# A gated recurrence with a highway layer on one Trainium2 core: the leftover tokens on 96 partitions, another order of the loads inside a tile, and a new instruction list

## The chip, the cores and the metric

The kernel runs on one core of a Trainium2 chip. The metric is device time in microseconds (us) of one execution; lower is better. Inputs and output are in HBM, in float32.

The engines are named as the profile names them. PE is the matrix engine, and PEld its weight loads. DVE, ACT and POOL are the three elementwise engines. SP computes nothing and only issues transfers. Transfers (DMA) are carried out by 16 DMA engines; the profile calls the share of their time that is busy the DMA share, with 1 for all 16.

## What is computed

```
sig = 1 / (1 + exp(-f_logit))                # f_logit, x: (4, 6336, 256)
f = lower_bound + (1 - lower_bound) * sig    # lower_bound: (256)
h = 0
for t in range(6336):                        # per batch and channel
    h = f[:, t] * h + (1 - f[:, t]) * x[:, t];  y[:, t] = h
y = y.reshape(25344, 256)
H = max(y @ w_h, 0);  T = 1 / (1 + exp(-(y @ w_t + b_t)))
out = T * H + (1 - T) * y                    # (25344, 256)
```

The recurrence runs along the tokens of a batch; the four batches are independent. The two inputs and the output have 25.95 MB each.

## The kernel before, in words

**Units.** The tokens are cut into 29 units (UNITS). Each row names k, the runs of tokens (batch, first token, number), the split of the product e between two engines, and how the steps are grouped. Most units are one run of 1024 tokens with k = 8; the first five and the last two are shorter (256 or 512 tokens). Since 6336 is not a multiple of 1024, one unit differs from the rest: unit 15 takes 192 tokens of each of the four batches, 768 tokens, with k = 6.

**Token layout.** A unit is loaded with k neighbouring tokens on each of the 128 partitions: token p*k + j lies on partition p, place j. A full unit is a load of 1 MB for f_logit (tile l) and one of 1 MB for x (tile x), in which each partition receives 8 KB that are contiguous in HBM. Unit 15 has 32 partitions for each batch and 6 KB on each partition. Its HBM side is a pattern with the four batches outermost (`in_dram`, line 219).

**Steps of a unit n**, each named by a letter in the list OPS:

- l, x: the two loads, and o: the stores (two of 512 KB for a full unit). All are issued by SP (lines 223 and 381).
- U (ACT, line 259): u = sigmoid(-l). B (POOL, line 281; DVE in the first two units, line 279): bv = u*x.
- T (PE, line 287): u is transposed, so that channels lie on partitions and tokens along a row; k transposes of 128 columns for each of the two halves h of the channels. F (ACT, line 297): f is made out of the transposed u; its read pattern (`token_order`, line 225) puts the tokens into their natural order. V (PE, line 305): the same transpose for bv, written in the natural order directly, two tokens at a time.
- S (DVE, line 313): the recurrence along the tokens. It needs the last column of the unit before in the same batch.
- Z and G (PE, line 324): the two products with the weights. A (ACT, line 335): the gate t. D (DVE, line 339): d = max(...) - y. E (DVE, line 345) and P (POOL, line 352): e = d*t, in two parts.
- O (PE, lines 363 and 364): y and e are transposed back and added, in PSUM (the accumulator memory that PE writes). C (ACT, line 376): the result is copied to the tile o, which the store sends out.

**Order.** OPS is one long written list. Each engine works through its own items in exactly that order, and SP issues loads and stores in that order too, each after the waits that its buffers need. The part behind the @ names the buffer: there are four l and four x buffers, three u and three bv, five y, eight o, four PSUM banks s and two double banks pp. X items are matmuls on zeros that only keep PE busy early on.

Of the kernel before, what the change touches and what calls it, by code (L numbers as in the profile page):

```python
# [36 lines left out]
    (6, ((0, 3072, 192), (1, 3072, 192), (2, 3072, 192), (3, 3072, 192)), 384, (4, 2), (2, 2, 2), (4, 2), ()),  # L37
# [23 lines left out]
X4@s0 Tb@s0 cst l0@l0 x0@x0 W1 W0 U0.0@u0 B0.0@bv0 X1@s1 T0.0@s1 T0.1@s2 F0.1@f0 F0.0@f1 w1 l1@l1 U1.0@u1  # L61
V0.0@s3 V0.1@s0 dia v1 S0.0@y0 X7@s2 T1.0@s2 S0.1 w0 v0 l2@l2 x1@x1 F1.0@f2 U2.0@u2 T1.1@s1 X3@pp0 Z0.0@pp0
X1@s3 T2.0@s3 F1.1@f3 A0.0@t0 B1.0@bv1 V1.1@s2 S1.1@y1 T2.1@s0 G0.0@pp1 Z0.1@pp0 V1.0@s1 D0.0@d0 X1@pp1
G0.1@pp1 S1.0 F2.0@f1 F2.1@f0 A0.1 x2@x2 B2.0@bv2 l3@l3 l4@l0 U3.0@u0 x3@x3 l5@l1 B3.0@bv0 X1@pp0 Z1.1@pp0
D0.1 A1.1@t1 U4.0@u1 G1.1@pp1 D1.1@d1 V2.0@s3 T3.1@s2 T3.0@s0 Z1.0@pp0 G1.0@pp1 S2.0@y2 F3.1@f3 F3.0@f2
V2.1@s1 S2.1 X1@s3 T4.1@s3 T4.0@s2 F4.1@f1 A1.0 F4.0@f0 D1.0 E1@e0 E0@e1 X4@pp1 G2.0@pp1 D2.0@d1 x4@x0 x5@x1
l6@l2 U5.0@u2 V3.0@s0 Z2.1@pp0 V3.1@s1 O0.0@s3 Z2.0@pp1 S3.0@y3 S3.1 A2.1@t1 A2.0 T5.1@s2 T5.0@s0 G2.1@pp0
C0.0@o0 F5.1@f2 D2.1 B4.0@bv1 B5.1@bv2 B5.0 Z3.0@pp1 V4.0@s1 O1.0@s3 Z3.1@pp0 V4.1@s2 A3.0@t0 F5.0@f3 A3.1
U6.0@u0 G3.1@pp1 G3.0@pp0 C1.0@o1 S4.0@y4 S4.1 D3.1@d0 D3.0 E2@e1 E3@e0 x6@x2 l8@l3 l7@l0 x7@x3 x8@x0 o0.0
o1.0 l9@l1 x9@x1 Z4.0@pp1 V5.0@s1 T6.0@s0 S5.0@y0 A4.0@t1 F6.0@f0 B6.0@bv0 B6.1 Z4.1@pp0 A4.1 O2.0@s2 O3.1@s3  # L70
C3.1@o2 U8.0@u1 C2.0@o3 V5.1@s0 G4.1@pp1 T6.1@s3 G4.0@pp0 S5.1 D4.0@d1 D4.1 V6.0@s1 U7.0@u2 F6.1@f1 Z5.0@pp0
T8.1@s0 V6.1@s2 Z5.1@pp1 S6.0@y1 B7.1@bv1 B7.0 A5.0@t0 F8.1@f3 A5.1 O3.0@s3 G5.1@pp0 T7.1@s1 S6.1 D5.1@d0
T7.0@s0 G5.0@pp1 E4@e0 D5.0 F7.1@f2 C3.0 F7.0@f0 Z6.1@pp0 V7.0@s2 A6.1@t1 U9.0@u0 O2.1@s1 O4.1@s3 V7.1@s0
Z6.0@pp1 B8.0@bv2 B8.1 S7.0@y3 S7.1 E5@e1 A6.0 T8.0@s2 G6.1@pp0 G6.0@pp1 T9.0@s0 C2.1 C4.1@o4 F8.0@f1 F9.0@f0
O4.0@s1 V8.1@s3 O5.2@s2 C4.0 C5.2@o5 l13@l2 l10@l3 U10.0@u2 x10@x2 l11@l0 D6.0@d1 D6.1 B9.1@bv0 B9.0 S8.1@y2
E6@e0 G7.1@pp1 T9.1@s0 O5.1@s1 Z7.0@pp0 D7.1@d0 T10.1@s2 V8.0@s3 C5.1@o6 F9.1@f2 A7.0@t0 F10.1@f3 O5.0@s1 C5.0
U11.0@u1 V9.0@s0 G7.0@pp0 Z7.1@pp1 O6.1@s2 C6.1@o7 x11@x3 o3.0 l12@l1 l17@l3 x12@x0 x13@x1 o2.0 S8.0 B10.0@bv1
B10.1 B11.1@bv2 O5.3@s1 D7.0 T11.0@s3 V9.1@s2 A7.1 P7.0@e1 B11.0 Z8.1@pp0 F11.0@f1 C5.3 A8.1@t1 S9.0@y4 S9.1
Z8.0@pp1 O6.3@s3 O6.2@s1 A8.0 T10.0@s0 G8.1@pp0 G8.0@pp1 O6.0@s2 C6.3@o0 U13.0@u0 C6.2 C6.0 F10.0@f0 D8.1@d1
D8.0 E7 E8@e0 V10.1@s3 Z9.0@pp0 S10.1@y0 O7.3@s1 A9.0@t0 C7.3@o1 T11.1@s2 F11.1@f2 V10.0@s0 G9.1@pp1 O7.0@s1  # L80
C7.0@o2 D9.1@d0 U12.0@u2 Z9.1@pp0 O7.2@s3 C7.2 S10.0 V11.0@s2 G9.0@pp1 V11.1@s1 O7.1@s3 T13.0@s0 A9.1 C7.1
F13.0@f3 Z10.1@pp0 D9.0 P8.0 B13.0@bv0 B13.1 B12.1@bv1 P9.0@e1 B12.0 T12.0@s3 G10.0@pp1 O8.2@s0 A10.1@t1
Z10.0@pp0 F12.0@f0 C8.2@o3 A10.0 l14@l0 o6.0 x17@x2 o7.0 o5.0 x14@x3 l15@l2 O8.3@s3 C8.3 x15@x1 o8.1 o4.0
S11.0@y1 D10.0@d1 S11.1 O8.1@s2 O8.0@s0 C8.1@o7 C8.0 U14.0@u1 G10.1@pp1 T13.1@s3 G11.1@pp0 T12.1@s2 D10.1 E9
E10@e0 D11.1@d0 V12.0@s1 Z11.0@pp1 O9.3@s0 S12.0@y3 F12.1@f1 F13.1@f2 A11.0@t0 C9.3@o2 Z11.1@pp0 O9.0@s2
V12.1@s3 S12.1 C9.0@o6 A11.1 B14.1@bv2 P10.0 B14.0 U15.0@u0 V13.0@s0 O9.2@s1 C9.2 O9.1@s2 G11.0@pp1 C9.1
U17.0@u2 G12.0@pp0 T14.1@s3 V13.1@s1 o8.0 l16@l1 o5.1 x16@x0 o9.0 x18@x3 l19@l0 D11.0 D12.0@d1 B15.0@bv1
P11.0@e1 S13.1@y2 S13.0 E11 Z12.1@pp1 G12.1@pp0 F14.1@f0 T15.1@s2 T14.0@s3 O10.3@s1 A12.1@t1 Z12.0@pp1
F14.0@f1 C10.3@o3 V14.0@s3 O10.1@s1 O10.2@s0 A12.0 Z13.1@pp1 C10.1@o4 F15.1@f2 A13.1@t0 C10.2 O11.2@s1
O10.0@s2 D12.1 S14.0@y4 B17.1@bv0 B15.1 P12.0@e0 G13.1@pp0 D13.1@d0 C11.2@o7 C10.0 U16.0@u1 O11.3@s0 T15.0@s1  # L90
V14.1@s3 C11.3 O11.0@s2 F15.0@f3 C11.0@o5 Z13.0@pp1 G13.0@pp0 O11.1@s0 A13.0 B16.1@bv2 S14.1 D13.0 E12 E13@e1
P13.0 B16.0 B17.0 T16.0@s1 T17.1@s3 V15.0@s2 C11.1 F16.0@f1 F17.1@f0 o9.1 l18@l2 o7.1 o6.1 l24@l3 o11.1 l20@l1
x19@x1 o10.1 S15.0@y0 Z14.1@pp0 Z14.0@pp1 O12.3@s0 V15.1@s1 O12.0@s3 T17.0@s2 A14.1@t1 C12.3@o6 A14.0 S15.1
G14.1@pp0 O12.1@s0 G14.0@pp1 D14.1@d1 D14.0 O12.2@s1 C12.0@o2 U18.0@u0 C12.2 C12.1 F17.0@f3 G15.1@pp0 V16.0@s3
P14.0@e0 D15.1@d0 S16.0@y1 E14 Z15.1@pp1 O13.2@s1 C13.2@o1 T16.1@s0 F16.1@f2 O13.0@s2 Z15.0@pp0 V16.1@s1
C13.0@o0 A15.1@t0 A15.0 V17.0@s0 O14.0@s3 C14.0@o7 S16.1 G15.0@pp1 O13.3@s2 O14.2@s3 O13.1@s1 D15.0 U19.0@u2
C13.3 B18.0@bv1 B18.1 P15.0@e1 B19.1@bv2 S17.0@y3 C13.1 C14.2@o3 Z16.0@pp0 G16.0@pp1 A16.0@t1 T18.0@s2
V17.1@s1 T18.1@s3 O14.1@s0 D16.0@d1 S17.1 F18.0@f1 G16.1@pp0 Z16.1@pp1 F18.1@f2 C14.1 A16.1 V18.0@s2 T19.1@s3
T19.0@s0 O14.3@s1 F19.1@f3 C14.3 F19.0@f0 D16.1 E15 E16@e0 S18.0@y2 P16.0 B19.0 Z17.0@pp1 V18.1@s3 O15.1@s1
G17.1@pp0 O15.0@s0 o12.1 l22@l2 o13.0 o11.0 x20@x0 l21@l0 o12.0 o14.1 x23@x2 x22@x3 x21@x1 o10.0 D17.1@d0  # L100
S18.1 A17.0@t0 C15.1@o6 U20.0@u1 C15.0 G17.0@pp1 O16.0@s2 C16.0@o0 Z17.1@pp0 A17.1 D17.0 T20.1@s1 O16.2@s0
O15.2@s2 V19.0@s3 B20.0@bv0 B20.1 P17.0@e1 Z18.0@pp0 C16.2@o5 C15.2@o2 F20.1@f1 A18.0@t1 G18.0@pp1 O16.3@s0
C16.3 O16.1@s2 V19.1@s1 S19.0@y4 D18.0@d1 S19.1 E17 U21.0@u0 Z18.1@pp0 V20.1@s3 T20.0@s0 G18.1@pp1 A18.1 C16.1
F20.0@f2 Z19.0@pp0 D18.1 S20.1@y0 B21.1@bv1 B21.0 P18.0@e0 A19.0@t0 O17.0@s1 T21.1@s2 F21.1@f0 U22.0@u2
V20.0@s0 G19.0@pp1 D19.0@d0 S20.0 G19.1@pp0 C17.0@o3 T21.0@s2 O17.3@s3 C17.3@o4 Z19.1@pp1 F21.0@f3 T22.1@s1
O17.1@s3 O17.2@s2 V21.1@s0 A19.1 D19.1 E18 E19@e1 o15.1 o15.0 x24@x0 l23@l1 l26@l0 C17.2 o17.1 o16.1 o16.0
S21.1@y1 Z20.1@pp1 C17.1 F22.1@f1 V21.0@s2 O18.1@s3 Z20.0@pp0 A20.1@t1 C18.1@o2 A20.0 S21.0 U23.0@u1 B22.0@bv2
P19.0 G20.0@pp1 O18.0@s1 O18.2@s3 G20.1@pp0 T22.0@s0 O18.3@s2 C18.0 C18.2@o6 C18.3 B22.1 D20.0@d1 D20.1
O19.2@s1 G21.1@pp1 U24.0@u0 F22.0@f2 C19.2@o4 D21.1@d0 B23.1@bv0 P20.0@e0 B23.0 x25@x1 l25@l2 o14.0 x26@x3
l28@l1 o17.0 o18.1 o13.1 o18.0 l27@l3 T23.0@s3 V22.1@s2 Z21.0@pp0 G21.0@pp1 V22.0@s0 A21.0@t0 S22.1@y3 S22.0  # L110
F23.0@f0 T24.0@s1 O19.3@s2 Z21.1@pp0 F24.0@f3 O19.1@s3 O19.0@s1 T23.1@s0 D21.0 A21.1 G22.0@pp0 C19.0@o5 C19.3
C19.1 F23.1@f1 E20 V23.0@s1 O20.2@s2 C20.2@o0 T24.1@s3 F24.1@f2 E21@e1 D22.0@d1 Z22.0@pp1 Z22.1@pp0 V23.1@s0
S23.0@y2 S23.1 B24.0@bv1 P21.0 B24.1 A22.0@t1 A22.1 O20.0@s2 C20.0@o7 U25.0@u2 O20.3@s3 G22.1@pp1 O21.0@s1
O21.3@s2 C21.3@o3 C21.0@o6 C20.3 G23.1@pp0 D22.1 D23.1@d0 B25.1@bv2 B25.0 O20.1@s0 V24.1@s2 T25.0@s1 C20.1
U26.0@u1 G23.0@pp1 V24.0@s3 T25.1@s0 P22.0@e0 S24.1@y4 D23.0 S24.0 E22 Z23.0@pp0 O21.2@s2 F25.1@f0 F25.0@f1
Z23.1@pp1 C21.2 V25.0@s0 O21.1@s1 V25.1@s2 A23.0@t0 A23.1 B26.1@bv0 B26.0 P23.0@e1 S25.1@y0 Z24.0@pp0 C21.1
U27.0@u0 A24.0@t1 G24.1@pp1 T26.1@s3 O22.2@s1 T26.0@s2 C22.2@o1 F26.0@f2 F26.1@f3 D24.1@d1 S25.0 Z24.1@pp0
T27.0@s1 G24.0@pp1 O22.3@s2 O22.1@s3 O22.0@s0 A24.1 C22.3 C22.1@o2 C22.0 F27.0@f0 Z25.0@pp0 V26.1@s2 D24.0 E23
E24@e0 x28@x2 x27@x0 o19.1 o19.0 o20.1 o20.0 o21.0 o22.0 o21.1 O23.2@s3 O23.0@s0 O23.3@s1 G25.0@pp1 A25.0@t0
C23.2@o4 C23.3 C23.0@o5 o23.1 o22.1 O23.1@s3 T27.1@s1 V26.0@s0 U28.0@u2 Z25.1@pp0 F27.1@f1 C23.1 S26.1@y1  # L120
P24.0 B27.0@bv1 B28.0@bv2 D25.0@d0 S26.0 A25.1 T28.1@s2 G25.1@pp1 T28.0@s1 O24.3@s3 G26.0@pp0 D25.1 D26.0@d1
# [10 lines left out]
def kernel(  # L132
# [66 lines left out]

    def need(key, n):  # L200
        if key not in st[n]:
            k = UNITS[n][0]
            shape, dt = {
                "l": ([P, 8, D], FP32), "x": ([P, 8, D], FP32), "u": ([P, 8, D], FP16), "bv": ([P, 4, D, 2], BF16),
                "f0": ([P, 8 * P], FP16), "f1": ([P, 8 * P], FP16), "y": ([P, NH, 8 * P], BF16),
# [222 lines left out]
```

## Time and profile before

| | us |
|---|---|
| median of 3 runs | 236.07 (235.56 to 237.6) |
| the profiled execution, its own time | 238.39 |
| its span, first to last instruction | 236.6 |

| engine | busy us | share of the span |
|---|---|---|
| PE | 201.3 | 85% |
| ACT | 201.0 | 85% |
| DVE | 197.5 | 83% |
| POOL | 151.2 | 64% |

The core moved 52.43 MB out of HBM and 25.95 MB into it, 331 GB/s over the span. Three things in the page help in reading it. The strip of 40 slices cuts the span into pieces of 5.9 us; a digit is a busy share in tenths. PEclk is the clock that was granted to PE, in tenths of full speed. The view of waits names, for the idle time ahead of an instruction, what came last of all that it waited for. A transfer is complete when the last of the DMA engines that carry it is done, and an engine that waits for a transfer waits for that.

### The profile page before, as it was taken

The page shows a single profiled execution, that of the slowest core. Times are in us where ns is not written, and L with a number is a line of the kernel's source. Part 1 is how long each engine was busy: PE and PEld are TensorE (multiplying, and loading weights), DVE is VectorE, ACT ScalarE, POOL GpSimd, SP SyncE. Part 2 cuts the span into 40 slices and gives each one's busy share as a digit, 9 for nine tenths or more (in the row PEclk, how much of TensorE's full clock was granted, in tenths as well). Part 3 has the DMA queues.
Part 4 walks back from the last instruction along what each step waited for, and adds up shares of the span by engine and source line. Part 5 has one row for each costly group of instructions (what it writes and reads, how often), then busy time and mean ns, then how long its engine had stood idle before and what let it go on. Part 6 is the DMA issues. An engine that isn't in the chain of part 4 may idle for free.

```text
span 236.6 us, 4629 instructions
## 1 busy us (share of the span) xinstructions
PE 201.3 (85%) x1818; PEld 141.1 (60%) x1818; DVE 197.5 (83%) x163; ACT 201.0 (85%) x248; POOL 151.2 (64%) x80
## 2 busy tenths in 40 slices
PE   7779889899999980688986969999949999999991
PEld 3356556576677660366664756766636777686771
DVE  3488999999999990394996988999946999999970
ACT  5799999999999940959949879999667999998892
POOL 2066568579889680049698637919887299878400
PEclk9999999999999998589999999999976999999999
DMA  6999999999999999559999599989999949547286
GB/s 210 350 423 421 417 414 421 418 420 419 419 418 334 382 208 232 180 171 332 425 425 377 208 346 345 425 320 427 375 341 416 375 179 346 222 159 288 107 336 269
DMA packets 16221, 78.68 MB, mean 333 GB/s; under 512 B 1732, under 2 KB 2248, under 8 KB 10824
## 3 DMA queue, kind: packets, MB, share of 16 engines
q1 hardware_dynamic: 16192, 78.39, 86.8%
q8 instruction: 14, 0.23, 0.4%
q14 instruction: 7, 0.06, 0.1%
q10 hardware_dynamic: 8, 0.00, 0.0%
HBM read 52.43 MB, written 25.95 MB: 331 GB/s over the span
## 4 chain that ended last, share of the span: by engine, by line
DMA 34%; PE 33%; DVE 19%; issue 6%; SPq 2%; POOL 2%; ACT 1%; ACTq 0%; DVEq 0%; POOLq 0%
DMA out_dram<-o 25%; DVE y L313 11%; DMA l<-in_f_logit_dram 9%; PE gp L324 8%; PE zp L324 8%; DVE d L339 7%; PE op L364 5%; PE op L363 4%; PE bT L305 4%; PE uT L287 4%; SPq L223 2%; DVE e L345 2%; ACT o L376 1%; POOL e L352 1%; POOL bv L281 1%
## 5 line engine op out<-in xcount | busy, mean ns | idle before, releaser
L281 POOL TENSOR_TENSOR bv<-u,x 128x1024 bf16<-128x1024 f16 (+1 forms) x49 | 103.9, 2138 | 58.6 <-DMA x<-in_x_dram 38.3
L313 DVE TENSOR_TENSOR_SCAN y<-f,y,bT 128x1024 bf16<-128x1024 f16 (+3 forms) x56 | 103.8, 1878 | 13.6 <-ACT o L376 9.1
L339 DVE SCALAR_TENSOR_TENSOR d<-y,ncc,gp 128x1024 bf16<-128x1024 bf16 (+3 forms) x58 | 63.6, 1112 | 11.1 <-PE gp L324 6.4
L376 ACT COPY o<-op 128x512 f32<-128x512 f32 x99 | 59.0, 651 | 6.9 <-DMA out_dram<-o 4.9
L259 ACT ACTIVATE u<-l 128x2048 f16<-128x2048 f32 (+3 forms) x29 | 49.9, 1721 | 16.2 <-DMA l<-in_f_logit_dram 16.1
L335 ACT ACTIVATE t<-zp,bt 128x1024 bf16<-128x1024 f32 (+3 forms) x58 | 60.4, 1056 | 3.2 <-issue 1.7
L363 PE MATMUL op<-diag,y 128*128 128x128 f16 x396 | 56.8, 224 | 6.6 <-ACT o L376 5.5
L297 ACT ACTIVATE f<-uT,ncc 128x1024 f16<-128x1024 f16 (+3 forms) x58 | 59.3, 1050 | 3.0 <-PE uT L287 3.0
L324 PEld LDWEIGHTS <-w_sb 128*128 128x128 f16 x408 | 38.5, 100 | 35.5 <-issue 10.5
L364 PE MATMUL op<-ident_b,e 128*128 128x128 bf16 x396 | 56.8, 226 | 2.0 <-DVE e L345 1.1
L364 PEld LDWEIGHTS <-e 128*128 128x128 bf16 x396 | 49.7, 142 | 13.0 <-issue 9.1
L352 POOL TENSOR_TENSOR e<-d,t 128x1152 bf16<-128x1152 bf16 (+1 forms) x20 | 46.9, 2345 | 14.6 <-DVE e L345 9.3
L324 PE MATMUL gp<-y,w_sb 128*128 128x512 bf16 (+1 forms) x204 | 53.3, 382 | 1.7 <-ACT t L335 0.9
L324 PE MATMUL zp<-y,w_sb 128*128 128x512 bf16 (+1 forms) x204 | 53.1, 380 | 1.4 <-ACT t L335 0.5
L363 PEld LDWEIGHTS <-y 128*128 128x128 bf16 x396 | 51.3, 143 | 4.5
L305 PE MATMUL bT<-ident_f,bv 128*128 128x128 f32 x198 | 32.9, 284 | 10.5 <-ACT o L376 9.1
L287 PE MATMUL uT<-ident_h,u 128*128 128x128 f16 x396 | 31.4, 224 | 5.5 <-ACT o L376 1.8
L287 PEld LDWEIGHTS <-u 128*128 128x128 f16 x396 | 26.6, 101 | 14.9 <-issue 5.1
L305 PEld LDWEIGHTS bT<-ident_f,bv 128*128 128x128 f32 x198 | 23.4, 145 | 17.3 <-ACT o L376 9.8
L345 DVE TENSOR_TENSOR e<-d,t 128x896 bf16<-128x896 bf16 (+4 forms) x29 | 21.2, 752 | 1.7 <-PE op L364 1.0
L313 DVE TENSOR_TENSOR_SCAN y<-f,bT 128x1024 bf16<-128x1024 f16 (+2 forms) x8 | 12.5, 1604 | 0.0
L386 PE MATMUL zeros<-zeros 128*128 128x512 bf16 x23 | 8.3, 471 | 2.7 <-DVE zeros L174 1.2
(25 smaller groups left out, 11.8 us busy)
## 6 DMA issues: line engine op xcount, KB each, us to landing
out_dram<-o SPq DMA_DIRECT2D x48, 512.0 KB, 10.0
l<-in_f_logit_dram SPq DMA_DIRECT2D x21, 1024.0 KB, 15.8
x<-in_x_dram SPq DMA_DIRECT2D x21, 1024.0 KB, 14.8
l<-in_f_logit_dram SPq DMA_DIRECT2D x5, 512.0 KB, 10.6
x<-in_x_dram SPq DMA_DIRECT2D x5, 512.0 KB, 9.0
out_dram<-o SPq DMA_DIRECT2D x3, 256.0 KB, 13.2
l<-in_f_logit_dram SPq DMA_DIRECT2D x1, 768.0 KB
x<-in_x_dram SPq DMA_DIRECT2D x1, 768.0 KB
```

What stands on the lines that cost most here:

```text
L259: pin(nc.scalar.activation(need("u", n)[:, :k], st[n]["l"][:, :k], AF.Sigmoid, scale=-1.0))
L281: on_pool(pin(nc.gpsimd.tensor_mul(o, u, v)))
L287: pin(nc.tensor.transpose(t[:, j * P:(j + 1) * P], st[n]["u"][:, j, h * P:(h + 1) * P], ident_h))
L297: pin(nc.scalar.activation(a, b, AF.Identity, scale=ncc[:, h:h + 1], bias=1.0))
L305: pin(nc.tensor.transpose(w[:, g], v[:, g, h * P:(h + 1) * P, 0], ident_f))
L313: pin(nc.vector.tensor_tensor_scan(y[:, h, c:c + m], st[n][f"f{h}"][:, c:c + m], st[n]["bT", h][:, c:c + m], 0.0 if prev is None else prev ...
L324: pin(nc.tensor.matmul(p[:, a:e], w_sb[:, k, ki, m * P:(m + 1) * P], st[n]["y"][:, ki, a:e], start=ki == 0, stop=ki == NH - 1))
L335: pin(nc.scalar.activation(need("t", n)[:, m, :N], st[n]["zp", m][:, :N], AF.Sigmoid, bias=bt[:, m:m + 1]))
L339: pin(nc.vector.scalar_tensor_tensor(need("d", n)[:, m, :N], st[n]["y"][:, m, :N], ncc[:, m:m + 1], st[n]["gp", m][:, :N], op0=ALU.mult, o ...
L363: pin(nc.tensor.matmul(o, st[n]["y"][:, h, j:k * P:k], diag[:, h], start=True, stop=False))
L364: pin(nc.tensor.matmul(o, st[n]["e"][:, h, j:k * P:k], ident_b, start=False, stop=True))
L376: pin(nc.scalar.copy(st[n]["o", s][:, j0 - base:j1 - base].rearrange("p j d -> p (j d)"), st[n]["op", q][:, :(j1 - j0) * D]))
```

## The change

Three things change together.

1. Unit 15 has k = 8 instead of 6. Its 768 tokens lie on 96 partitions instead of 128, two tokens of each of the four batches on each partition. In its loads and stores the partition is the outermost dimension on both sides; on the HBM side, each piece has 2 KB. All steps of this unit use 96 partitions where tokens lie on partitions. It now has four groups in O and C (it had three), two equal stores of 384 KB (it had one of 512 and one of 256 KB), and 448 columns of e on DVE instead of 384.
2. In the loads of every other unit the runs of k tokens are dealt out differently: run number i*16 + e goes to partition e*8 + i (it was partition i*16 + e). Pieces and sizes stay as they were. F's read pattern and V's write pattern undo the new order; S and all that follows see the natural order, as before. The stores of these units are unchanged.
3. OPS is a new list. It has the same steps (but for unit 15's additional O and C, and X items), the same buffers, and another order of them throughout, that of the loads and stores included. It begins with the load of unit 1, ahead of that of unit 0.

```diff
-    (6, ((0, 3072, 192), (1, 3072, 192), (2, 3072, 192), (3, 3072, 192)), 384, (4, 2), (2, 2, 2), (4, 2), ()),
+    (8, ((0, 3072, 192), (1, 3072, 192), (2, 3072, 192), (3, 3072, 192)), 448, (4, 4), (2, 2, 2, 2), (4, 4), ()),
...
-X4@s0 Tb@s0 cst l0@l0 x0@x0 W1 W0 U0.0@u0 B0.0@bv0 X1@s1 T0.0@s1 T0.1@s2 F0.1@f0 F0.0@f1 w1 l1@l1 U1.0@u1
+l1@l0 X4@s0 Tb@s0 l0@l1 cst dia U1@u0 x0@x0 U0@u1 X3@s1 T0.1@s1 T1.0@s2 T0.0@s3 F0.1@f0 F0.0@f1 F1.0@f2
...
-    def in_dram(ap, n):
+    def shape(n):
         k, runs = UNITS[n][:2]
-        (b, a, m), q = runs[0], len(runs)
-        if q == 1:
-            return ap[b, a:a + m, :].rearrange("(p j) d -> p j d", j=k)
-        assert [(r, a, m) for r in range(b, b + q)] == list(runs)
-        return ap[b:b + q, a:a + m, :].rearrange("b (p j) d -> b p j d", j=k)
+        r = len(runs)
+        b, a, m = runs[0]
+        assert [(b + i, a, m) for i in range(r)] == list(runs) and m * r % k == 0
+        return m * r // k, k, r, k // r, m * r
+
+    def copy(n, tile_, dram, to_dram=False, j0=0, j1=None):
+        np_, k, r, kr, _ = shape(n)
+        j1 = k if j1 is None else j1
+        b, a, m = UNITS[n][1][0]
+        t = tile_[:np_, :j1 - j0]
+        if r == 1:
+            d = dram[b, a:a + m, :].rearrange("(p j) d -> p j d", j=kr)[:, j0:j1]
+        else:
+            d = dram[b + j0 // kr:b + j1 // kr, a:a + m, :].rearrange("b (p j) d -> p b j d", j=kr)
+            t = t.rearrange("p (b j) d -> p b j d", j=kr)
+        pin(nc.sync.dma_start(d, t) if to_dram else nc.sync.dma_start(t, d))
 
     def load(key, src, n):
-        k = UNITS[n][0]
-        pin(nc.sync.dma_start(need(key, n)[:, :k], in_dram(src, n)))
-
-    def token_order(ap, n, inner):
-        k = UNITS[n][0]
-        return ap.rearrange("c (j p) -> c p j", j=k) if inner else ap.rearrange("c (p j) -> c p j", j=k)
+        _, k, r, kr, _ = shape(n)
+        if r > 1:
+            return copy(n, need(key, n), src)
+        b, a, m = UNITS[n][1][0]
+        d = src[b, a:a + m, :].rearrange("(i e j) d -> e i (j d)", e=16, j=kr)
+        pin(nc.sync.dma_start(need(key, n)[:, :k].rearrange("p j d -> p (j d)"), d))
...
     def op_F(n, h):
-        a, b = token_order(f[:, :N], n, False), token_order(st[n]["uT", h][:, :N], n, True)
+        if r == 1:
+            a = f[:, :N].rearrange("c (i e j) -> c i e j", e=16, j=kr)
+            b = st[n]["uT", h][:, :N].rearrange("c (j e i) -> c i e j", e=16, j=kr)
+        else:
+            a = f[:, :N].rearrange("c (b p j) -> c b p j", b=r, j=kr)
+            b = st[n]["uT", h][:, :N].rearrange("c (b j p) -> c b p j", b=r, j=kr)
...
     def op_V(n, h):
-        w = t.bitcast(FP32)[:, :k * P // 2].rearrange("c (p g) -> c g p", g=k // 2)
         for g in range(k // 2):
-            pin(nc.tensor.transpose(w[:, g], v[:, g, h * P:(h + 1) * P, 0], ident_f))
+            b, i = divmod(2 * g, kr)
+            w = t.bitcast(FP32)[:, b * np_ * kr // 2:(b + 1) * np_ * kr // 2]
+            w = w[:, i // 2::kr // 2]
+            if r == 1:
+                w = w.rearrange("c (i e) -> c e i", e=16)
+            pin(nc.tensor.transpose(w, v[:np_, g, h * P:(h + 1) * P, 0], ident_f[:np_, :np_]))
...
     def op_o(n, s):
-        pin(nc.sync.dma_start(in_dram(out_bsd, n)[..., j0:j1, :], st[n]["o", s][:, :j1 - j0]))
+        copy(n, st[n]["o", s], out_bsd, True, j0, j1)
```

## The prediction, made before the changed kernel was run

> **What bounds the kernel now.** I read the page's strip first, then tables of busy time by stretch, then the waits around the worst stretch. The strip shows where the time is lost. Its digits stand for 40 slices of 5.9 us.
>
> ```profile
> DVE  3488999999999990394996988999946999999970
> ACT  5799999999999940959949879999667999998892
> PEclk9999999999999998589999999999976999999999
> DMA  6999999999999999559999599989999949547286
> GB/s 210 350 423 421 417 414 421 418 420 419 419 418 334 382 208 232 180 171 332 425 425 377 208 346 345 425 320 427 375 341 416 375 179 346 222 159 288 107 336 269
> ```
>
> Counted from 0: up to slice 13 DVE, ACT and the DMA engines are all near 9, so three resources end together. At slices 14 and 15 ACT and DVE stop, although the DMA engines are still called busy, and from 14 to 17 the rate is half. Around slice 29 there is a second, smaller stop. The tables by stretch put numbers to it; after the stretch and its length stand the busy times of PE, PEld, DVE, ACT and POOL (instructions in brackets), PE's granted clock, the DMA share, and GB/s.
>
> ```profile
> 20.00:84.00 64.00, 59.20 (x552) 41.62 (x550) 63.57 (x47) 63.86 (x73) 50.05 (x24) 1.00 0.99 403
> 84.00:108.00 24.00, 13.70 (x99) 8.91 (x99) 13.52 (x9) 11.75 (x13) 7.88 (x4) 0.79 0.77 210
> 108.00:132.00 24.00, 20.32 (x203) 15.42 (x204) 19.34 (x19) 20.31 (x26) 20.82 (x11) 1.00 1.01 391
> 132.00:152.00 20.00, 18.14 (x176) 12.68 (x175) 17.99 (x13) 17.43 (x22) 12.25 (x7) 1.00 0.85 317
> 152.00:176.00 24.00, 19.34 (x184) 13.96 (x183) 22.11 (x15) 20.39 (x23) 16.84 (x9) 0.96 0.97 369
> 176.00:200.00 24.00, 23.73 (x209) 17.16 (x207) 20.67 (x14) 22.34 (x27) 18.28 (x9) 0.89 0.86 327
> 200.00:220.00 20.00, 19.99 (x194) 14.49 (x193) 19.77 (x15) 18.89 (x27) 16.38 (x8) 1.00 0.56 221
> 220.00:236.60 16.60, 11.59 (x131) 9.01 (x129) 9.54 (x12) 11.15 (x20) 2.39 (x1) 0.97 0.64 254
> ```
>
> From 20 to 84 us DVE and ACT idle for 0.43 and 0.14 us of 64. So the undisturbed kernel is bound by its engines, with the DMA engines just keeping up. From 84 to 220 us DVE idles for 10.48 + 4.66 + 2.01 + 1.89 + 3.33 + 0.23 = 22.6 us, ACT for 12.25 + 3.69 + 2.57 + 3.61 + 1.66 + 1.11 = 24.9 us. Finer stretches show why.
>
> ```profile
> 100.00:102.00 2.00, 2.00 (x11) 1.15 (x10) 2.00 (x2) 1.24 (x2) 0.00 (x0) 0.50 0.26 105
> 102.00:104.00 2.00, 2.00 (x22) 1.48 (x19) 2.00 (x3) 1.11 (x1) 0.32 (x1) 0.86 0.25 102
> 134.00:136.00 2.00, 2.00 (x18) 1.37 (x17) 2.00 (x2) 1.12 (x3) 1.42 (x1) 1.00 0.26 104
> 192.00:194.00 2.00, 2.00 (x22) 1.55 (x21) 2.00 (x2) 2.00 (x3) 2.00 (x2) 1.00 0.26 107
> ```
>
> A share of 0.25 is 4 of 16 DMA engines, and 104 GB/s is a quarter of 420. Unit 15's HBM pattern has the 4 batches outermost, and this is its mark: its transfers run on four engines. Two loads of 768 KB and stores of as much put 2.36 MB on four engines, 23 us at 104 GB/s, where sixteen at 420 need 5.6. Later transfers queue behind this on the same four, and each is complete only with its last engine, so the lag is handed on: four engines are still catching up at 134 and at 192 us. The waits from 80 to 112 us and two rows of the timeline show who pays.
>
> ```profile
> POOL bv L281 <- DMA x<-in_x_dram: 16.1, 1, 16.1
> ACT u L259 <- DMA l<-in_f_logit_dram: 9.5, 1, 9.5
> DVE y L313 <- ACT o L376: 9.1, 1, 9.1
> ```
>
> ```profile
> 94.97 1.48 ACT L259 ACTIVATE u<-l 128x1536 f16<-128x1536 f32 x1 [9.48 <-DMA l<-in_f_logit_dram]
> 103.68 2.16 POOL L281 TENSOR_TENSOR bv<-u,x 128x1024 bf16<-128x1024 f16 x1 [16.12 <-DMA x<-in_x_dram]
> ```
>
> The 128x1536 tile is unit 15's. ACT stands before it, behind that the copies which free PSUM, and behind those DVE's next recurrence. POOL waits for unit 15's x.
>
> **The change part by part.** The sum starts from the profiled span, 236.6 us. That execution's own time is 238.39, 1.8 more than the span; the median of the runs is 236.07, 1.0% less.
>
> Unit 15's transfers. With 96 partitions outermost on both sides all 16 DMA engines can share them. What goes is the idle time of 84 to 220 us, as far as it stems from the four slow engines. Lower bound: only the stall that ends on unit 15's own loads, DVE's 10.48 us. Upper bound: all of it, which leaves 236.6 - 22.6 = 214.0 by DVE and 236.6 - 24.9 = 211.7 by ACT. I take DVE's whole 22.6, since from 20 to 84 us the same steps run without idling, and the later gaps end on transfers or on a PE at half clock, which came after each of the two stops (0.50 in the rows at 100 us and from 175 to 177 us).
>
> What is late next: no engine can go below its work. So I put back an idling of 0.23 in 20 us (the row at 200) to 1.11 in 20 (ACT, same row) over the 113 us that are left of the 136: 1.3 to 6.3, taken at 2.5, nearer to DVE, whose sum is the longer. 214.0 + 2.5 = 216.5.
>
> Unit 15's engine work. U on 128x2048 takes 1.97 us, on 128x1536 1.48: +0.49 on ACT. One more copy of 0.65: ACT +1.1 in all. The second bv is full size, 2.16 instead of 1.17: POOL +1.0, and POOL idles for a third of the span. PE gets 4 + 2 + 8 = 14 more matmuls at the 0.06 us that separate such matmuls in the timeline, +0.8. S, D and A run along 768 tokens as before; 64 columns of e move from POOL to DVE, under 0.1 us. ACT's sum becomes 211.7 + 1.1 = 212.8, still under DVE's 214.0, so I add nothing; the bounds are 0 and 1.1.
>
> [...] The rows price only the steps that have tokens on partitions, and those leave 216.5.
>
> The new deal of the loads. Sizes and pieces stay; only the addresses that are read at one time change. Before, no row shows this pattern for the big loads. The nearest is that of the two weight loads, whose 128 rows of 1 KB follow each other in HBM. From 5 to 6 us, beside the first x, the rate was 352 GB/s, and the trace's packet records give medians of 46, 84, 159 and 313 ns for 1, 2, 4 and 8 KB, so the weights' 1 KB packets cost no more than their size says. I take 0. Upper bound: slow reads as they occur before; see the third rival. A gain is not excluded but small: from 20 to 82 us the rate was 407 GB/s at a share of 1.00, and the best slice has 427, 5% more, on transfers that the engines' work already covers.
>
> [...] No run here shows which engine serves which partition. [...]
>
> F's and V's new patterns read and write as many elements; 0, with PE's slack (59.2 of 64 us) over V.
>
> The new list. Every instruction is moved, each queue included. Its start: DVE idles for 9.0 of the first 20 us, 1.65 of them for the second x. Loading unit 1 first brings one f_logit forward and lets another slip; bounds -2 and +1.5, taken as 0. The end: the same last units and a final store, DVE 7.06 us idle after 220; 0, +-1.
>
> Are the transfers still hidden? 78.68 MB at 407 GB/s take 193 us; 216.5 leaves 23 for the start and the end. Yes, but with a tenth to spare.
>
> Sum: span 216.5, own time 218.3, and 1.0% less for the median: 216.
>
> **The rivals.** *Slow reads stay.* After 84 us there are stretches at full share and low rate, such as this:
>
> ```profile
> 144.00:146.00 2.00, 1.96 (x23) 1.36 (x21) 2.00 (x2) 2.00 (x3) 2.00 (x2) 1.00 0.98 256
> ```
>
> All engines are busy here and slow. I put it down to engines out of step after unit 15, as there is none from 20 to 82 us; but the profile does not prove it, and the new list can leave gaps of its own. If only the 10.48 us go: span 226.1, median 225 to 226.
>
> *The transfers of unit 15 still run on few engines.* Its pieces of 2 KB come from four batches. Then nothing is gained: 234 to 238. Against it: partitions are outermost, as in all transfers that reach 420 GB/s.
>
> *The new deal reads slowly* (the other side). If 16 engines that read neighbouring addresses get in each other's way, all loads slow down. With 10 us of start and end and the 25.95 MB of stores at 407 GB/s (64 us), reading at r GB/s gives a span of 74 + 52430/r. From r = 367 down this exceeds 216.5, from 322 down it exceeds 236.6; at 300 it is 249, median 248. For it: rows of 256 and less exist. Against it: the weights' rows.
>
> **How the numbers follow.** My forecast, 211 to 220: 0.62. Slow reads or gaps stay, 220 to 232: 0.22. Few engines, 234 to 238: 0.05. Slow deal or a list that loses as much, above 238: 0.11. The predicted time is 216. Leaving out the last two gives the range 211 to 232; the low end takes the start's 2 us, 2 of the 2.5 put back and the end's 1; the high end is 226 with the 6.3 us that ACT's row gives. A measurement of this kernel tells about 1% from no change: faster 0.62 + 0.22 = 0.84, same 0.05, slower 0.11.
>
> **What would show it.** Right: no stretch at a share of 0.25 with 104 GB/s while loads are pending; unit 15's U not waiting for its load; no drop of the granted clock in mid-span; ACT and DVE idle for under 5 us each from 84 us to 16 us before the end. Wrong: loads at full share below 367 GB/s from 20 to 80 us, or ACT and DVE waiting there, where they did not before.

## The result and the profile after

The changed kernel takes 272.14 us (median of 4 runs, 266.9 to 281.32), the kernel before 236.45 in the same comparison. The ratio is 1.136, 95% interval 1.121 to 1.151: slower, where 216 us and a gain were forecast. The ratio counts the less disturbed runs of each kernel, and is so a little below that of the medians; the profile below is of an execution of 273.92 us.

The strip of the changed kernel, in slices of 6.8 us:

```profile
DVE  2569556379083889529919999998997648999981
ACT  4765853871747969389399999959969389999884
PEclk9999967599575999959979999999999959999999
DMA  6999999999999999999999999999999999962477
GB/s 171 254 246 231 230 229 228 231 228 251 244 247 256 237 290 243 302 356 403 258 333 396 378 387 388 338 294 381 354 311 293 347 363 382 338 268 106 168 297 308
```

In mid-span there is no slice at half a DMA share any more: unit 15's four-engine stretch is gone. (The low slices from 35 on are the end of the kernel.) But from the first slices on the DMA engines are called busy all the time and move some 230 GB/s, where they moved 420 before. DVE and ACT, both at 9 in these slices before, now run in bursts. Three stretches of 60 us, and the waits of the first of them (us in total, times, longest; line numbers are the changed kernel's):

```profile
20.00:80.00 60.00, 36.62 (x251) 23.01 (x253) 37.81 (x30) 33.62 (x37) 25.94 (x12) 0.80 1.03 234
80.00:140.00 60.00, 44.87 (x376) 31.87 (x383) 41.17 (x28) 44.45 (x51) 39.29 (x18) 0.87 1.02 292
140.00:200.00 60.00, 56.54 (x545) 41.34 (x552) 55.32 (x45) 56.53 (x69) 41.87 (x20) 0.98 1.02 368
```

```profile
POOL bv L290 <- DMA x<-in_x_dram: 27.9, 5, 9.5
ACT u L269 <- DMA l<-in_f_logit_dram: 23.6, 6, 7.5
DVE d L355 <- PE gp L340: 12.5, 4, 6.6
```

In the first stretch ACT works for 33.6 of 60 us and waits 23.6 for loads of f_logit; POOL waits 27.9 for x. PE works for 36.6 us, at a mean granted clock of 0.80 (before, from 20 to 84 us, it had 1.00), and DVE waits for it. So the loads set the time, at a DMA share of 1.03: all 16 engines are occupied and slow. This is the sign of being wrong that the prediction had named: loads at full share below 367 GB/s from 20 to 80 us. The later stretches, which hold more stores, are faster, at the same share. The trace's packet records say the same: over the whole span an 8 KB packet takes 528 ns in the median, 313 before, and a 4 KB packet (most of them stores) 159 in both.

### The profile page after: what moved, and what is told of

Read it like the earlier page. It is cut to its first block, busy times and chain, and to the rows that moved or that the text cites. A ratio compares the mean times of both kernels' runs of the same rounds, so it can differ in the third digit from the quotient of the medians.

```text
span 272.1 us, 4633 instructions
## 1 busy us (share of the span) xinstructions
PE 212.2 (78%) x1803; PEld 147.6 (54%) x1833; DVE 199.5 (73%) x163; ACT 203.8 (75%) x249; POOL 154.1 (57%) x80
## 5 line engine op out<-in xcount | busy, mean ns | idle before, releaser
L329 DVE TENSOR_TENSOR_SCAN y<-f,y,bT 128x1024 bf16<-128x1024 f16 (+3 forms) x56 | 103.8, 1880 | 12.4 <-PE bT L322 10.2
L380 PE MATMUL op<-diag,y 128*128 128x128 f16 (+1 forms) x400 | 59.4, 230 | 10.8 <-ACT o L394 10.3
L340 PEld LDWEIGHTS <-w_sb 128*128 128x128 f16 x408 | 40.6, 105 | 46.4 <-issue 22.6
L394 ACT COPY o<-op 128x512 f32<-128x512 f32 (+1 forms) x100 | 56.4, 614 | 11.1 <-DMA out_dram<-o 6.8
L381 PE MATMUL op<-ident_b,e 128*128 128x128 bf16 (+1 forms) x400 | 59.6, 232 | 2.0 <-POOL e L367 1.5
L381 PEld LDWEIGHTS <-e 128*128 128x128 bf16 (+1 forms) x400 | 51.2, 143 | 17.8 <-issue 12.5
L367 POOL TENSOR_TENSOR e<-d,t 128x1152 bf16<-128x1152 bf16 (+1 forms) x20 | 47.3, 2365 | 22.6 <-DVE e L361 18.5
L380 PEld LDWEIGHTS <-y 128*128 128x128 bf16 (+1 forms) x400 | 52.4, 144 | 6.0 <-issue 1.1
L322 PE MATMUL bT<-ident_f,bv 128*128 128x128 f32 (+1 forms) x200 | 33.3, 288 | 15.0 <-POOL bv L290 10.3
L296 PE MATMUL uT<-ident_h,u 128*128 128x128 f16 (+1 forms) x400 | 33.5, 233 | 10.9 <-ACT u L269 7.7
L296 PEld LDWEIGHTS <-u 128*128 128x128 f16 (+1 forms) x400 | 28.2, 105 | 19.7 <-ACT u L269 11.9
L322 PEld LDWEIGHTS bT<-ident_f,bv 128*128 128x128 f32 (+1 forms) x200 | 23.2, 148 | 21.9 <-POOL bv L290 13.2
L361 DVE TENSOR_TENSOR e<-d,t 128x896 bf16<-128x896 bf16 (+3 forms) x29 | 21.9, 770 | 5.3 <-ACT t L351 5.3
```

What stands on the lines that cost most here:

```text
L296: pin(nc.tensor.transpose(t[:, j * np_:(j + 1) * np_], st[n]["u"][:np_, j, h * P:(h + 1) * P], ident_h[:np_, :np_]))
L322: pin(nc.tensor.transpose(w, v[:np_, g, h * P:(h + 1) * P, 0], ident_f[:np_, :np_]))
L329: pin(nc.vector.tensor_tensor_scan(y[:, h, c:c + m], st[n][f"f{h}"][:, c:c + m], st[n]["bT", h][:, c:c + m], 0.0 if prev is None else prev ...
L340: pin(nc.tensor.matmul(p[:, a:e], w_sb[:, k, ki, m * P:(m + 1) * P], st[n]["y"][:, ki, a:e], start=ki == 0, stop=ki == NH - 1))
L380: pin(nc.tensor.matmul(o, st[n]["y"][:, h, cols], diag[:, h], start=True, stop=False))
L381: pin(nc.tensor.matmul(o, st[n]["e"][:, h, cols], ident_b, start=False, stop=True))
```

## The experiments

The first question was which of the three parts costs the time; the second, why. Times are medians of 4 runs, and each ratio is to the kernel before on the same chip (237.68, 238.32 and 238.21 us in the three comparisons).

### 1. The changed kernel with the loads dealt out as before

```diff
     def load(key, src, n):
-        _, k, r, kr, _ = shape(n)
-        if r > 1:
-            return copy(n, need(key, n), src)
-        b, a, m = UNITS[n][1][0]
-        d = src[b, a:a + m, :].rearrange("(i e j) d -> e i (j d)", e=16, j=kr)
-        pin(nc.sync.dma_start(need(key, n)[:, :k].rearrange("p j d -> p (j d)"), d))
+        copy(n, need(key, n), src)          # F's and V's patterns go back with it
```

> The changed kernel with only the loads dealt out as before (run p to partition p); 96 partitions in unit 15 and the new list stay. Theory, that the new deal alone slows the loads (230 GB/s from 20 to 80 us in the changed kernel's trace, 407 before): the loads return to about 410 GB/s, nothing stops on unit 15, and the time is what the prediction's sum gave, 211 to 222 us. Rival, that the new list or the 96 partitions cost the time: it stays at 255 to 275 us.

Measured: 214.45 us, ratio 0.904 (0.898 to 0.910). The same stretches:

```profile
20.00:80.00 60.00, 53.72 (x497) 38.30 (x505) 59.54 (x44) 59.50 (x66) 47.59 (x23) 1.00 1.01 418
80.00:140.00 60.00, 58.22 (x577) 43.27 (x585) 59.60 (x47) 60.00 (x74) 47.44 (x23) 1.00 1.02 384
140.00:200.00 60.00, 58.77 (x555) 43.27 (x564) 59.39 (x43) 58.17 (x75) 49.49 (x23) 1.00 0.83 330
```

DVE idles for 0.46, 0.40 and 0.61 us of 60, and PE's clock is full in all three. By the two ratios the new deal costs 1.136 - 0.904 = 0.232 of the time before, some 55 us (57.7 by the medians, which come from different comparisons). The rest of the change gains 10%; this is the lowest median of the study, with those of experiment 4 within 1.3 us. F's and V's patterns went back together with the loads, so this run does not tell them apart; experiment 4 does, since it keeps such patterns and is as fast.

### 2. The kernel before with the new deal alone

```diff
+        if len(runs) > 1:                   # unit 15 as before
+            return pin(nc.sync.dma_start(need(key, n)[:, :k], in_dram(src, n)))
+        d = src[b, a:a + m, :].rearrange("(i e j) d -> e i (j d)", e=16, j=k)
+        pin(nc.sync.dma_start(need(key, n)[:, :k].rearrange("p j d -> p (j d)"), d))
```

> The kernel before with only the new deal of the loads in all units but 15; list, unit 15 and its four-engine transfers as before. Theory (the new deal slows the loads): about 230 GB/s from 20 to 80 us, and a time of 262 to 290 us, since the stops of unit 15 come on top. Rival (list or 96 partitions): 234 to 240 us, 400 GB/s and more from 20 to 80 us.

Measured: 307.52 us, ratio 1.293 (1.283 to 1.302).

```profile
20.00:80.00 60.00, 38.79 (x265) 25.32 (x268) 40.99 (x31) 33.54 (x38) 25.95 (x12) 0.83 1.02 231
```

The slow loads come with the deal, under either list, and here they cost 69.8 us. The time is 17 us over the top of what was expected; that slow loads and unit 15's stops add up to more than I had allowed is likely, but was not tried.

### 3. The kernel before with unit 15's transfers cut by batch

```diff
+        for i in range(q):                  # loads; the stores likewise
+            pin(nc.sync.dma_start(t[i * P // q:(i + 1) * P // q, :k], in_dram(src, n)[i]))
```

> The kernel before with unit 15's loads and stores issued as one transfer per batch (32 partitions each), so that each can use all 16 DMA engines; everything else as before. Theory of the prediction's first step (the four-engine transfers cause the stops after 84 us): no stretch at a share of 0.25 while loads are pending, and 213 to 222 us. Rival (slow reads that have nothing to do with unit 15 cause the later gaps): only the stop at 88 to 98 us goes, 225 to 229 us.

Measured: 221.15 us, ratio 0.931 (0.924 to 0.938). The two stretches that held the stop, and their successors:

```profile
84.00:108.00 24.00, 23.15 (x226) 16.86 (x228) 23.68 (x23) 23.02 (x28) 22.01 (x11) 1.00 1.02 400
108.00:132.00 24.00, 20.79 (x200) 15.15 (x200) 20.80 (x15) 21.58 (x26) 15.91 (x8) 1.00 1.01 402
132.00:152.00 20.00, 18.76 (x176) 13.57 (x179) 19.90 (x14) 19.97 (x25) 14.26 (x7) 1.00 0.95 370
152.00:176.00 24.00, 20.78 (x205) 15.56 (x207) 21.98 (x16) 20.91 (x25) 22.36 (x11) 1.00 1.00 382
```

Nothing else was changed, and 16.5 us are gone: DVE works for 23.68 of the 24 us in which it had worked for 13.52. So the four-engine transfers caused the stop and most of what followed. A few us of gaps stay under the old list (DVE 3.2 in the second row).

### 4. The new deal as 64x2 and as 32x4

```diff
-        d = src[b, a:a + m, :].rearrange("(i e j) d -> e i (j d)", e=16, j=kr)
+        d = src[b, a:a + m, :].rearrange("(i e j) d -> e i (j d)", e=64, j=kr)     # second run: e=32
```

> [...] Theory A (the addresses: engines that read within 128 KB get in each other's way in HBM): 400 GB/s and more from 20 to 80 us, 211 to 224 us. Theory B (not the addresses but the form: where the outermost counts of the two sides differ, the partitions are shared out among the engines in another way, and engines collide where they write): about 230 GB/s and 255 to 275 us.

> The changed kernel with the deal 32x4 instead of 16x8: run i*32 + e goes to partition 4e + i, so that pieces of 8 KB from neighbouring runs are still read in a row, but 32 is the outermost count. Loads alone in this deal ran at 422 GB/s. Both theories that are left: 418 GB/s or so from 20 to 80 us and 213 to 217 us. If it stays above 225 us, the rate of loads alone does not carry over to the kernel.

Measured: 215.48 us (ratio 0.908, 0.903 to 0.913) and 215.71 us (0.904, 0.898 to 0.911); both load at 418 GB/s from 20 to 80 us, which is this row of the first:

```profile
20.00:80.00 60.00, 53.75 (x493) 38.09 (x502) 59.06 (x44) 59.50 (x66) 47.42 (x22) 1.00 1.01 418
```

Both keep F's and V's patterns in the same kind as the changed kernel, so these patterns are not what costs the time. By what I had written, 64x2 spoke for the addresses (theory A): I supposed that under 64x2 the pieces read at one time lie further apart, which no run here shows. That conclusion fell with the next runs: theory B had assumed that any outermost count other than 128 is shared out alike, and 16 loads at 234 GB/s, 32 and 64 at 418.

### 5. The new list with unit 15 on four engines again

In the kernel of experiment 1, unit 15's HBM pattern has the batches outermost again, on 96 partitions: 24 partitions of 8 tokens for each batch, so its pieces have 8 KB instead of 2.

```diff
-            d = dram[b + j0 // kr:b + j1 // kr, a:a + m, :].rearrange("b (p j) d -> p b j d", j=kr)
-            t = t.rearrange("p (b j) d -> p b j d", j=kr)
+            d = dram[b:b + q, a:a + m, :].rearrange("b (p j) d -> b p j d", j=kr)[:, :, j0:j1]
```

> The kernel of the first experiment (new list, loads dealt out as before) with unit 15 on 96 partitions but with the batches outermost in its loads and stores again, so that they run on four engines: 24 partitions of 8 tokens for each batch. Theory (the four engines cause the stops, whatever the list): a stretch at a share of 0.25, stops of 10 us and more after unit 15's loads, 225 to 240 us. Rival (the new list is what removes the stops, by loading unit 15 earlier against its use): 213 to 219 us.

Measured: 228.43 us, ratio 0.956 (0.951 to 0.961), and 14.0 us more than experiment 1 (12.4 by the ratios, since the two stand in different comparisons). In the stretch of the stop:

```profile
94.00:98.00 4.00, 1.17 (x9) 0.95 (x9) 1.19 (x1) 3.60 (x4) 1.15 (x1) 0.75 0.35 145
98.00:102.00 4.00, 3.78 (x16) 2.00 (x16) 0.71 (x1) 3.69 (x5) 0.00 (x0) 0.50 0.97 264
```

DVE works for 1.9 of 8 us and PE's clock falls to 0.50, as before. The list does not remove the stop; the transfer's form does. But the list is not worth nothing: with the four engines kept, list and 96 partitions together take 9.9 us off the kernel before (238.32 to 228.43).

### 6. Loads alone, without compute

A kernel that only loads x into 16 tiles, in groups of 16 loads, and fills the output with zeros. Its groups show each form by itself.

> Loads alone: no compute, the output is filled with zeros at the end. Twelve groups of 16 loads of x into 16 tiles, each group drained before the next: (1) natural deal, 1 MB; (2) the changed kernel's deal 16x8, (3) 32x4, (4) 64x2, all with pieces of 8 KB; deal 16x8 with pieces of (5) 7 KB, (6) 9 KB, (7) 4 KB; (8) natural partitions, eight pieces of 1 KB that lie 128 KB apart for each partition; (9) four pieces of 2 KB, 256 KB apart; (10) unit 15 on 96 partitions; (11) unit 15 as before, batches outermost; (12) unit 15 by batch on 32 partitions. Theory W (engines read too close together): rates follow the distance of the pieces read at one time: (1) and (4) 410 to 425 GB/s, (2) 220 to 240, (3) between, (5) and (6) as slow as (2), (7) slower than (2). Theory P (distances that are powers of two collide): (5) and (6) are 380 GB/s and more, since 7 and 9 KB and their multiples are no powers of two. If (2) alone runs at 400, neither holds and the slowness needs the other traffic of the kernel. For unit 15: (11) at 100 to 107 GB/s, four engines; (10) and (12) are open, between 200 and 390.

One row inside each group, in the order of the list above; the last number is GB/s, the one ahead of it the DMA share:

```profile
10.00:40.00 30.00, 0.00 (x0) 0.00 (x0) 1.00 1.01 423
55.00:115.00 60.00, 0.00 (x0) 0.00 (x0) 1.00 1.01 221
135.00:160.00 25.00, 0.00 (x0) 0.00 (x0) 1.00 1.01 423
180.00:205.00 25.00, 0.00 (x0) 0.00 (x0) 1.00 1.02 424
225.00:270.00 45.00, 0.00 (x0) 0.00 (x0) 1.00 1.02 224
295.00:360.00 65.00, 0.00 (x0) 0.00 (x0) 1.00 1.01 221
380.00:400.00 20.00, 0.00 (x0) 0.00 (x0) 1.00 1.03 234
420.00:455.00 35.00, 0.00 (x0) 0.00 (x0) 1.00 1.10 348
475.00:500.00 25.00, 0.00 (x0) 0.00 (x0) 1.00 1.05 387
520.00:555.00 35.00, 0.00 (x0) 0.00 (x0) 1.00 1.06 261
590.00:680.00 90.00, 0.00 (x0) 0.00 (x0) 1.00 0.25 106
700.00:735.00 35.00, 0.00 (x0) 0.00 (x0) 1.00 1.02 234
```

The deal 16x8 halves the rate with nothing else running. Theory P falls: with 7 and 9 KB pieces it is as slow. Theory W is in trouble: 32x4 is not between but at the full rate, while a plain transfer to 32 partitions, with contiguous reads, is slow too. And the rate is nearly the same for pieces of 4, 7, 8 and 9 KB (234, 224, 221, 221), so what is halved is a bandwidth, and no fixed time is added to each piece.

### 7. Loads alone, addresses against form

W says that the addresses in HBM decide, F that the form does: the outermost count of the HBM side.

> Loads alone again (no compute; the output is filled with zeros), in groups that set the addresses in HBM against the form. After the first such run (16x8 at 221 GB/s whatever the piece, 32x4 and 64x2 at 422, 32 partitions at 235) two theories are left. W: engines that read within 128 to 192 KB of HBM get in each other's way. [...] Groups: (1) natural, 1 MB: 422 by both. (2) 16x8 in form, but each engine's 8 pieces of 8 KB follow each other and engines are 72 KB apart: W 420, F 220. (3) 32x4 with pieces of 4 KB, all within 128 KB: W 235 or less, F 400 and more. (4) 64x2 with pieces of 2 KB within 32 KB twice: W 235 or less, F 370 and more. (5) 128 partitions with pieces of 1 KB, 128 KB in all: W below 240, F 300 and more. (6) and (7) partitions 0 to 63 and 64 to 127 alone, natural: W 420, F 215 to 240. (8) the two halves by turns: W 420, F between 220 and 420. (9) stores in the 16x8 form: open.

One row inside groups 1 to 4 and 6 to 9:

```profile
10.00:40.00 30.00, 0.00 (x0) 0.00 (x0) 1.00 1.01 423
55.00:110.00 55.00, 0.00 (x0) 0.00 (x0) 1.00 1.02 234
131.00:138.00 7.00, 0.00 (x0) 0.00 (x0) 1.00 1.03 416
154.00:158.00 4.00, 0.00 (x0) 0.00 (x0) 1.00 1.04 388
182.00:212.00 30.00, 0.00 (x0) 0.00 (x0) 1.00 1.01 205
226.00:256.00 30.00, 0.00 (x0) 0.00 (x0) 1.00 1.02 207
272.00:336.00 64.00, 0.00 (x0) 0.00 (x0) 1.00 1.01 217
346.00:370.00 24.00, 0.00 (x0) 0.00 (x0) 1.00 1.01 423
```

This settles W against F. The second row has spread-out reads (each of the 16 outermost entries reads 64 KB in a row, 72 KB from the next) and the 16x8 form: 234. The third has the 32x4 form, with the 32 pieces of one step within 128 KB: 416. So it is the form. (Group 5, only 2 MB, is too short for a rate of its own.) The rows of 64 partitions (205 and 207), whose loads differ from those of the first row in writing 64 partitions, 512 KB, instead of 128, have about half the first row's 423, and the 221 to 234 of the 16x8 form lie a little above them. Which engine writes which partition is not in the trace, so whether one limit is behind both is not shown. The last row shows that it is a matter of loads: a store in the 16x8 form runs at 423.

### 8. Loads and stores by turns

> Loads of x and stores of zeros by turns, no compute, to see why the changed kernel's loads run at 234 GB/s from 20 to 80 us, when there are few stores, and its transfers at 368 later. Groups: (1) 16 natural loads of 1 MB, a store of 512 KB behind each; (2) the same with the loads in the deal 16x8; (3) as (2), each store split into two of 256 KB. If loads and stores simply add (4.7 us for a load at 221 GB/s, 1.2 for a store at 422): (1) 422, (2) and (3) 263 GB/s. If stores pull the engines out of step and the collisions go: (2) and (3) 330 GB/s and more.

Rows of group 1, group 2, and four rows along group 3:

```profile
8.00:60.00 52.00, 0.00 (x0) 0.00 (x0) 1.00 1.02 422
76.00:146.00 70.00, 0.00 (x0) 0.00 (x0) 1.00 1.02 274
186.00:206.00 20.00, 0.00 (x0) 0.00 (x0) 1.00 1.02 281
206.00:218.00 12.00, 0.00 (x0) 0.00 (x0) 1.00 1.02 306
218.00:226.00 8.00, 0.00 (x0) 0.00 (x0) 1.00 1.02 338
228.00:238.00 10.00, 0.00 (x0) 0.00 (x0) 1.00 1.02 415
```

Group 2 is near the plain sum (263). Group 3 starts so too, and then climbs to 415 GB/s with nothing changed in what is issued; its 8 KB packets fall from 565 ns in the median (166 to 206 us) to 309 in the packet records, with about two 2 KB packets of stores to each of them all along. So the loss can dissolve by itself; why is not shown, nor what starts the recovery. The changed kernel recovers too, from 234 GB/s to 368 from 140 us on; that the cause is the same was not tried.

## Why the prediction was wrong, point by point

**The failed step is "The new deal of the loads", where I took 0.** It costs some 55 us: the loads run at 234 GB/s from 20 to 80 us, and no longer at the 403 to 407 before. I chose the nearest row by its addresses: the weights, read within a short stretch of HBM. But the weights' transfers have 128 outermost on both sides, and the outermost count, not the distance, decides (experiment 7: 234 GB/s with 16 outermost and reads 72 KB apart, 416 with 32 outermost and all reads within 128 KB). No row of the kernel before showed a form with 16 outermost over 8; the honest bound was wide on the slow side, and the row that came nearest in form, unit 15's with 4 outermost over 32, was the one in trouble.

**The third rival named the right place and outcome, with the wrong mechanism.** It blamed neighbouring addresses. Pieces that lie within 128 KB are loaded at 416 GB/s in another form (experiment 7). Its price was too high as well: r = 230 gives a span of 74 + 52430/230 = 302 us, where the span is 272, since the rate rises to 292 and 368 in the later stretches; under the old list, with unit 15's stops on top, 307.52 was measured. Its chance of 0.11 was too low for a pattern that no row priced.

**What the loads write was not asked.** The prediction looked only at the addresses that are read. Loads to 64 of the 128 partitions run at 205 and 207 GB/s (experiment 7), so how many partitions a load writes counts as well.

**Unit 15's transfers: right in kind, too large in size.** The mark of four engines was read rightly: 0.25 and 106 GB/s by themselves in experiment 6. The landing records of the trace before show it too, and the lag that is handed on: unit 15's f_logit load has four, at 91.81, 92.50, 93.78 and 94.95 us, and U starts at 94.97. The store issued at 78.12 us has 16, twelve of them by 83.55 and the last four from 104.26 to 105.89, and the next store was issued at 105.90. But the form alone is worth 16.5 us under the old list (experiment 3) and 12 to 14 us under the new one (experiment 5), where I took all of the 22.6 us. Nor was the price of 104 GB/s the whole story of the stop: while ACT waited for unit 15's load, from 84 to 94 us, the share was 1.01 at 222 GB/s, and unit 15's 6 KB packets took 485 ns in the median (84 to 96 us), not the 238 that they took from 100 to 104 us at a share of 0.25.

The rival that the transfers stay on few engines is out. They do not reach 420, though: 261 GB/s alone on 96 partitions, 234 by batch on 32. In experiment 1 that stretch is short, and DVE works through it:

```profile
84.00:88.00 4.00, 3.85 (x40) 2.88 (x39) 4.00 (x4) 4.00 (x5) 2.92 (x2) 1.00 1.07 233
88.00:92.00 4.00, 3.75 (x37) 2.80 (x37) 4.00 (x4) 4.00 (x7) 3.65 (x2) 1.00 1.10 197
```

**The sum without the deal: the number is right, in part by luck.** It gave 216, and experiment 1 measured 214.45. Of the 2.5 us put back for idling DVE used 1.5 in the 180 us from 20 to 200; the start, taken at 0, gave little to see (DVE idles for 9.2 of the first 20 us, before 9.0). But the sum gave the whole gain to the four engines and nothing to the new list in mid-span. In the runs the list, with 96 partitions, brings 6.7 us (experiment 1 against 3) to 9.9 us (experiment 5), about as much as the four engines fall short of what I took. The list alone was not run. The price of unit 15's own steps held: in the changed kernel U took 1.91 us on 96x2048, where I had counted the 1.97 of 128x2048, and each half of bv 2.15 on 96x1024, where I had counted 2.16.

**Slow reads stay: half right.** Under the old list gaps remain (221.15 where the four engines alone are removed); with the new list and 96 partitions they are gone. The slow reads of the kernel before at full share (256 GB/s at 0.98 from 144 to 146 us) have rates like the half-rate forms; experiment 3 has most of them removed with the four engines, but why each occurred was not tried.

## What to carry to other kernels

A transfer is priced by its whole pattern on both sides, the outermost counts first: in these runs 4 outermost left a share of 0.25, and loads to all 128 partitions ran at half rate with 16 outermost, at the full one with 32, 64 or 128 (pieces of 4 KB and more). A share of 1.0 says nothing about the rate: it stood beside 221 as beside 423 GB/s. When a change gives a transfer a form that the trace has never shown, measure that form alone before building on it: one kernel of loads told twelve forms apart in a single run. And a change of three parts can hide a gain of 10% behind one number: with 32 or 64 in place of 16 the same deal runs 9% to 10% faster than before.

## What the runs showed of the hardware that was not expected

- In experiments 6 and 7, loads with 16 outermost over 8 run at 221 to 234 GB/s whatever the piece (4 to 9 KB), with 32 over 4 or 64 over 2 at 416 to 424 (388 with 64 over 2 and 2 KB pieces). Stores in the 16-over-8 form are not slowed: 423.
- There, loads to 64 partitions run at 205 to 207 GB/s, to 32 (the four quarters by turns) at 234, to 96 (2 KB pieces) at 261; the two halves by turns at 217, so a transfer to the other half does not fill the gap.
- The loss can end by itself: in experiment 8 one mix of loads and stores climbed from 281 to 415 GB/s within some 30 us while the same kinds of transfers were issued.
